# Gated linear attention with a SiLU MLP on one core: attention output with tokens on partitions and turned by transposes, results stored from ScalarE's queue

## The chip, the core and the metric

One NeuronCore of a Trainium2 chip runs the whole program. Its engines work side by side, each with its own instruction stream: TensorE (PE; its weight loads are listed apart as PEld), VectorE (DVE), ScalarE (ACT), GpSimd (POOL) and SyncE (SP), which here only issues transfers. Sixteen DMA engines move data between HBM and the on-chip memory SBUF; matmuls write to PSUM. The metric is the device time of one execution in microseconds (us), as a median over runs; lower is better.

## The reference

Inputs are q, k, v and f_logit of shape (4, 8, 768, 48), f32, and two weight matrices. What is computed:

```
f = 1.0 / (1.0 + np.exp(-f_logit))
state = np.zeros((B, H, D, D), dtype=np.float32)
for t in range(S):
    state = f[:, :, t, :, None] * state + np.einsum('bhd,bhe->bhde', k[:, :, t], v[:, :, t])
    y[:, :, t] = np.einsum('bhd,bhde->bhe', q[:, :, t], state)
x = y.transpose(0, 2, 1, 3).reshape(B * S, H * D)      # (3072, 384)
h = x @ w_in                                           # (3072, 2048)
g = h * (1.0 / (1.0 + np.exp(-h)))
out = g @ w_out                                        # (3072, 384)
```

## The kernel before

The 768 tokens are cut into six chunks of 128. Chunk g holds four units, one per batch entry b, and a unit is all eight heads of that entry. Heads are paired (four pairs) in most matmuls. For a chunk the work is:

- **prep(g)**: `logs` takes exp and log of the gate logits on ACT; `decay` sums the logs over the tokens by a matmul with a triangle of ones (tile `cs`, one PSUM buffer), takes two exponentials of the sum on ACT (`ia`, then `a`), and multiplies k by `ia` on POOL (`ki`) and q by `a` on DVE (`qg`). `values` converts v to bf16, and `lasts` gives the decay of the whole chunk (`al`).
- **attend(g)**, unit by unit and staggered: `transposes` (T) turns qg and ki by eight PE transposes and copies them out on DVE (`qk`); `scores` (A) makes the score tiles, which DVE masks into `atm`; `outputs` (Y) makes the attention output; `state` (D) updates the running state `st`.
- **mlp_in(g)** multiplies by w_in, 48 matmuls in 16 groups of three, each group followed by one SiLU on ACT (`hT`). **mlp_out(g)** multiplies by w_out, four tiles of 16 matmuls, recorded in groups of four; each finished tile is copied to `o_sb` (three buffers) and stored.

In `outputs` before, the result has features on partitions: `y_ps` is [128 features, 3, 128 tokens]. For each of the three feature blocks the kernel multiplies the heads that overlap the block; v sits zero-padded in `vp` (each head in a window of D + 128 columns) so that heads which straddle a block edge add only their own features, and `st` is kept at the full width of 384 columns with zeros off its diagonal blocks. A unit needs 10 matmuls against v and, from chunk 1 on, 6 against the state, all with 128 columns. One DVE copy makes `xT`, the operand of mlp_in.

The order of the work is written by hand: `run` interleaves generators, always taking the next step of the stream that has used the smallest share of its declared cost (`T_COST`, `A_COST`, `Y_COST`, `D_COST`, 650 for a group of the MLP, 200 for a unit of prep). Each engine then executes its own list strictly in that order. Chunk 1 is special: its first two units (FIRST) and its last two (SECOND) are handled apart, since their data still arrives while the MLP of chunk 0 runs. Names such as `logs(1, *SECOND)` say chunk and half.

All loads are issued from SP. In the kernel before, the stores of the results (L280) are issued from SP too, in program order among the loads; the weights come through POOL's queue (`load_w_in`, `load_w_out`). An engine's DMA instruction stands in its list like any other: what follows it waits until it has been issued.

PSUM tiles that matter: `cs`/`al_ps` share one buffer, `a_ps` and `t_ps` have one each, `y_ps` and `d_ps` share two ("yd"), `h_ps` and `o_ps` share two.

Of the kernel before, what the change touches and what calls it, by code (L numbers as in the profile page):

```python
# [41 lines left out]
def kernel(  # L42
# [20 lines left out]
    VW = D + 128  # L63
# [34 lines left out]
    vp = [singles.tile([C, B, 128 + H * VW], BF16, name=f"vp{i}") for i in range(2)]  # L98
    st = [singles.tile([C, NP, HD], BF16, name=f"st{i}") for i in range(B)]
# [93 lines left out]
    def outputs(g, b):  # L193
        i = g % 2
        y_ps = yps.tile([128, KT, C], F32, name="y_ps", tag="yd")
        for t in range(KT):
            terms = []
            if g > 0:
                for p in range(NP):
                    if 2 * D * p < 128 * (t + 1) and 2 * D * (p + 1) > 128 * t:  # L200
                        terms.append((st[b][:, p, 128 * t:128 * (t + 1)], qkT[b][:, 0, p, :]))
            for h in range(H):
                if D * h < 128 * (t + 1) and D * (h + 1) > 128 * t:
                    terms.append((v_window(i, b, h, t), atm[b][:, h % 2, h // 2, :]))
            for n, (l, r) in enumerate(terms):
                nc.tensor.matmul(y_ps[:, t, :], l, r, start=(n == 0), stop=(n == len(terms) - 1))  # L206
# [4 lines left out]
    def state(g, b):
        i = g % 2
        flat = st[b].rearrange("p n w -> p (n w)")
        blocks = bass.AP(flat.tensor, flat.offset, [list(flat.ap[0]), [HD + 2 * D, NP], [1, 2 * D]])
        d_ps = yps.tile([128, NP, 2 * D], F32, name="d_ps", tag="yd")
        if g > 0:
            nc.tensor.matmul(d_ps, ident, blocks, start=True, stop=False, skip_group_check=True)  # L217
        vv = v_data(i, b)
        for p in range(NP):
            nc.tensor.matmul(d_ps[:, p, :], ki[i][:, b, 2 * p:2 * p + 2, :], vv[:, 2 * p:2 * p + 2],  # L220
# [218 lines left out]
```

## Time and profile before

| what | us |
|---|---|
| median of 3 runs (lowest, highest) | 245.88 (244.97, 246.54) |
| the profiled execution's own time | 248.17 |
| its span, first to last instruction | 246.4 |
| PE / ACT / DVE / POOL busy in the span | 201.1 / 114.3 / 111.0 / 53.3 |
| mean granted TensorE clock | 0.924 of full speed |

The span is what the trace shows; 1.77 us of the execution lie around it. Times in the trace count from the span's start. A granted clock of 1.00 is 2.4 GHz, and 0.5 is 1.2 GHz. A busy PE is a union of overlapping matmuls, so what a matmul costs in a stream is read from the distance between starts, not from its own duration (a lone matmul's duration contains its way through the array).

### The profile page before, as it was taken

The page shows a single profiled execution, that of the slowest core. Times are in us where ns is not written, and L with a number is a line of the kernel's source. Part 1 is how long each engine was busy: PE and PEld are TensorE (multiplying, and loading weights), DVE is VectorE, ACT ScalarE, POOL GpSimd, SP SyncE. Part 2 cuts the span into 40 slices and gives each one's busy share as a digit, 9 for nine tenths or more (in the row PEclk, how much of TensorE's full clock was granted, in tenths as well). Part 3 has the DMA queues.
Part 4 walks back from the last instruction along what each step waited for, and adds up shares of the span by engine and source line. Part 5 has one row for each costly group of instructions (what it writes and reads, how often), then busy time and mean ns, then how long its engine had stood idle before and what let it go on. Part 6 is the DMA issues. An engine that isn't in the chain of part 4 may idle for free.

```text
span 246.4 us, 4049 instructions
## 1 busy us (share of the span) xinstructions
PE 201.1 (82%) x1680; PEld 123.4 (50%) x1680; DVE 111.0 (45%) x193; ACT 114.3 (46%) x181; POOL 53.3 (22%) x65
## 2 busy tenths in 40 slices
PE   0346689968604896899779999999999999999994
PEld 0125534536304672687535565655666555663462
DVE  7727722246204544467655345763557453520011
ACT  4351237850410386348265683556735654008600
POOL 8629100050300006300190000900009100000000
PEclk9999769999965798589958999999999999999999
DMA  8999999999992000699409991179601100100011
GB/s 138 187 186 194 191 185 190 197 180 185 189 192 95 0 3 32 131 188 176 85 28 195 187 137 49 49 141 188 90 35 64 36 0 0 63 37 32 3 64 64
DMA packets 105971, 27.00 MB, mean 110 GB/s; under 512 B 99296, under 2 KB 105952, under 8 KB 105952
## 3 DMA queue, kind: packets, MB, share of 16 engines
q1 hardware_dynamic: 102272, 23.60, 60.3%
q0 software_dynamic: 3680, 3.15, 7.9%
q8 instruction: 13, 0.21, 0.4%
q14 instruction: 6, 0.05, 0.1%
HBM read 25.17 MB, written 4.72 MB: 121 GB/s over the span
## 4 chain that ended last, share of the span: by engine, by line
PE 77%; DMA 6%; DVE 5%; ACT 4%; SPq 4%; issue 2%; ACTq 0%; DVEq 0%
PE h_ps L263 29%; PE o_ps L273 25%; PE y_ps L206 9%; PE t_ps L176 5%; SPq L85 4%; PE a_ps L186 3%; DMA out_dram<-o_sb 3%; DMA q_ld<-in_q_dram 3%; DVE atm L190 2%; ACT ia L144 2%; PE cs L142 2%; ACT a L147 2%; PE d_ps L220 2%; DVE qk L178 1%; PE d_ps L217 1%
## 5 line engine op out<-in xcount | busy, mean ns | idle before, releaser
L266 ACT ACTIVATE hT<-h_ps 128x512 bf16<-128x512 f32 x96 | 57.3, 597 | 64.0 <-PE h_ps L263 62.0
L263 PE MATMUL h_ps<-xT,w_in_sb 128*128 128x512 bf16 (+1 forms) x336 | 79.6, 373 | 0.9 <-DVE xT L209 0.7
L273 PE MATMUL o_ps<-w_out_sb,hT 128*128 128x384 bf16 x384 | 72.0, 330 | 0.0
L273 PEld LDWEIGHTS <-hT 128*128 128x128 bf16 x384 | 35.9, 99 | 27.7 <-issue 7.2
L263 PEld LDWEIGHTS <-w_in_sb 128*128 128x128 bf16 x336 | 32.6, 104 | 29.5 <-issue 9.0
L145 POOL TENSOR_TENSOR ki<-k_ld,ia 128x384 bf16<-128x384 f32 x24 | 26.3, 1094 | 67.5 <-ACT ia L144 26.8
L190 DVE TENSOR_TENSOR atm<-a_ps,triu 128x512 bf16<-128x512 f32 x48 | 30.9, 685 | 17.6 <-PE a_ps L186 17.4
L278 DVE COPY o_sb<-o_ps 128x384 f32<-128x384 f32 x24 | 13.4, 556 | 44.9 <-PE o_ps L273 32.5
L155 POOL CAST vp<-v_ld 128x384 bf16<-128x384 f32 x22 | 15.1, 691 | 70.3 <-DMA v_ld<-in_v_dram 70.3
L144 ACT ACTIVATE ia<-cs 128x384 f32<-128x384 f32 x24 | 11.8, 490 | 33.2 <-PE cs L142 33.2
L148 DVE TENSOR_TENSOR qg<-q_ld,a 128x384 bf16<-128x384 f32 x24 | 17.9, 754 | 16.9 <-ACT a L147 12.0
L178 DVE COPY qk<-t_ps 128x1024 bf16<-128x1024 bf16 x24 | 16.6, 690 | 18.0 <-PE t_ps L176 18.0
L142 PE MATMUL cs<-lf,triu 128*128 128x384 bf16 x24 | 8.9, 369 | 18.5 <-ACT a L147 10.2
L206 PE MATMUL y_ps<-atm,vp 128*128 128x128 bf16 x240 | 23.7, 234 | 0.1
L224 DVE TENSOR_TENSOR st<-d_ps,al 48x192 bf16<-48x192 f32 x40 | 14.2, 354 | 21.0 <-PE d_ps L220 17.0
L176 PE MATMUL t_ps<-ident,qg 128*128 128x128 bf16 x96 | 11.3, 252 | 15.0 <-DVE qg L148 11.7
L176 PEld LDWEIGHTS <-qg 128*128 128x128 bf16 x96 | 8.8, 115 | 21.6 <-DVE qg L148 13.8
L209 DVE CAST xT<-y_ps 128x384 bf16<-128x384 f32 x24 | 13.3, 555 | 12.3 <-PE y_ps L206 12.3
L206 PEld LDWEIGHTS <-vp 128*128 128x128 bf16 x240 | 17.8, 106 | 0.5 <-issue 0.5
L206 PE MATMUL y_ps<-qk,st 128*128 128x128 bf16 x120 | 16.5, 219 | 0.0
L186 PE MATMUL a_ps<-qk 48*128 48x128 bf16 x192 | 10.2, 230 | 6.0 <-DVE atm L190 6.0
L186 PEld LDWEIGHTS <-qk 48*128 48x128 bf16 x192 | 5.8, 99 | 15.5 <-issue 7.7
(37 smaller groups left out, 126.6 us busy)
## 6 DMA issues: line engine op xcount, KB each, us to landing
out_dram<-o_sb SPq DMA_DIRECT2D x24, 192.0 KB, 1.9
f_ld<-in_f_logit_dram SPq DMA_DIRECT2D x4, 768.0 KB, 11.0
k_ld<-in_k_dram SPq DMA_DIRECT2D x4, 768.0 KB, 6.4
q_ld<-in_q_dram SPq DMA_DIRECT2D x4, 768.0 KB, 10.1
v_ld<-in_v_dram SPq DMA_DIRECT2D x4, 768.0 KB, 11.1
f_ld<-in_f_logit_dram SPq DMA_DIRECT2D x4, 384.0 KB, 6.7
k_ld<-in_k_dram SPq DMA_DIRECT2D x4, 384.0 KB, 6.7
q_ld<-in_q_dram SPq DMA_DIRECT2D x4, 384.0 KB, 6.8
```

What stands on the lines that cost most here:

```text
L144: nc.scalar.activation(ia, cs, AF.Exp, scale=1.0)
L145: nc.gpsimd.tensor_mul(ki[i][:, b, :, 0:D], loaded[g, "k"][:, b], ia)
L148: nc.vector.tensor_mul(qg[i][:, b, :, 0:D], loaded[g, "q"][:, b], a)
L155: nc.gpsimd.tensor_copy(dst, src)
L176: nc.tensor.transpose(t_ps[:, j, p, :], src[i][:, b, 2 * p:2 * p + 2, :], ident)
L178: nc.vector.tensor_copy(sb, t_ps)
L186: nc.tensor.matmul(a_ps[:, r, p, :], qkT[b][lo:lo + D, 1, p, :], qkT[b][lo:lo + D, 0, p, :], start=True, stop=True)
L190: nc.vector.tensor_mul(sb[:, r], a_ps[:, r], triu[:, None, :].to_broadcast([C, NP, C]))
L206: nc.tensor.matmul(y_ps[:, t, :], l, r, start=(n == 0), stop=(n == len(terms) - 1))
L263: nc.tensor.matmul(h_ps[:, j], w_in_sb[:, kk, (n + j) * 128:(n + j + 1) * 128], xT[g][:, kk, lo:hi].rearrange("p b c -> p (b c)"), start=( ...
L266: nc.scalar.activation(hT[g][:, n:n + per, lo * C:hi * C], h_ps, AF.Silu)
L273: nc.tensor.matmul(o_ps, hT[g][:, n, b * C:(b + 1) * C], w_out_sb[:, n, :], start=(n == 0), stop=(n == NT - 1))
```

## The change

`outputs` now makes the attention output with tokens on partitions: `y_ps` is [128 tokens, 8 heads, 48]. Per pair there is one matmul against the state (moving operand `st`, 96 columns, from chunk 1 on) and two against v (moving operand `vb`, 48 columns). The result is copied to SBUF as bf16 (`y`), and a new step `turn` (X) makes three PE transposes of it into `x_ps` and copies these to `xT`. In `attend`, X of a unit stands one round after its Y. `vp` becomes the plain `vb`, `st` shrinks to 96 columns per pair, and their zero fills go or move to POOL.

The copy of each result tile and its store move to ACT (`nc.scalar.copy`, `nc.scalar.dma_start`), so that SP issues loads alone. In the opening, the first half runs through its scores before the second half's decays, the copies of chunk 0's outputs are ACT's, and both weights are requested in one place. The declared costs of prep rise from 320 to about 1000 per unit, and some leads are set anew.

```diff
-    vp = [singles.tile([C, B, 128 + H * VW], BF16, name=f"vp{i}") for i in range(2)]
-    st = [singles.tile([C, NP, HD], BF16, name=f"st{i}") for i in range(B)]
+    vb = [singles.tile([C, B, H, D], BF16, name=f"vb{i}") for i in range(2)]
+    st = [singles.tile([C, NP, 2 * D], BF16, name=f"st{i}") for i in range(B)]
...
+    def outputs(g, b, engine=None):
         i = g % 2
-        y_ps = yps.tile([128, KT, C], F32, name="y_ps", tag="yd")
+        y_ps = yps.tile([C, H, D], F32, name="y_ps", tag="yd")
+        opened = False
+        for p in range(NP):
+            if g > 0:
+                nc.tensor.matmul(y_ps[:, 2 * p:2 * p + 2, :], qkT[b][:, 0, p, :], st[b][:, p, :],
+                                 start=not opened, stop=False, skip_group_check=True)
+                opened = True
+            for r in range(2):
+                nc.tensor.matmul(y_ps[:, 2 * p + r, :], atm[b][:, r, p, :], vb[i][:, b, 2 * p + r, :],
+                                 start=not opened, stop=True, skip_group_check=True)
+                opened = True
+        sb = wk.tile([C, HD], BF16, name="y")
+        evac(engine, sb, y_ps.rearrange("p h d -> p (h d)"))
+        ysb[b] = sb
+
+    def turn(g, b, engine=None):
+
+        x_ps = yps.tile([128, KT, C], BF16, name="x_ps", tag="yd")
         for t in range(KT):
...
+            nc.tensor.transpose(x_ps[:, t, :], ysb[b][:, 128 * t:128 * (t + 1)], ident)
...
+        evac(engine, xT[g][:, :, b, :], x_ps)
...
-            nc.vector.tensor_copy(o_sb, o_ps)
+            nc.scalar.copy(o_sb, o_ps)
             r0 = b * S + g * C
-            nc.sync.dma_start(out=out[r0:r0 + C, :], in_=o_sb)
+            nc.scalar.dma_start(out=out[r0:r0 + C, :], in_=o_sb)
...
-            yield 200.0
+            yield 1000.0
...
+        for b in range(*FIRST):
+            transposes(0, b)
         logs(0, *SECOND)
         for b in range(*FIRST):
+            scores(0, b)
+        for b in range(*SECOND):
+            decay(0, b)
+        load_w_in()
+        load_w_out()
+        for b in range(*FIRST):
+            outputs(0, b, nc.scalar)
+        for b in range(*SECOND):
             transposes(0, b)
...
-        load(2, "f")
-
-
-        run((mlp_in(0, *ALL), mlp_cost(*ALL)), (states(0, *ALL), B * D_COST))
-        for name in "kqv":
+        for name in "fkqv":
             load(2, name)
         load(3, "f")
+
+
+        run((mlp_in(0, *ALL), mlp_cost(*ALL)), (states(0, *ALL), B * D_COST))
...
-        run((part(out0, 3900.0), 3900.0))
+        run((part(out0, 5850.0), 5850.0))
         run((part(out0, 1950.0), 1950.0), (prep(1, *FIRST), prep_cost(*FIRST)))
-        run((out0, mlp_cost(*ALL) - 5850.0), (attend(1, *FIRST), attend_cost(1, *FIRST)))
+        run((out0, mlp_cost(*ALL) - 7800.0), (attend(1, *FIRST), attend_cost(1, *FIRST)))
...
-            (chain(wait(3000.0), prep(2, *ALL)), 3000.0 + prep_cost(*ALL)))
+            (chain(wait(1000.0), prep(2, *ALL)), 1000.0 + prep_cost(*ALL)))
...
-                lead = half if g == 1 else 1300.0
+                lead = half if g == 1 else 2000.0
```

SP's list from the loads of chunk 2 on, before:

```order
L85 DMA f_ld<-in_f_logit_dram 128x32x48
L85 DMA k_ld<-in_k_dram 128x32x48
L85 DMA q_ld<-in_q_dram 128x32x48
L85 DMA v_ld<-in_v_dram 128x32x48
L85 DMA f_ld<-in_f_logit_dram 128x32x48
L280 DMA out_dram<-o_sb 128x384 x6
L85 DMA k_ld<-in_k_dram 128x32x48
```

and the same place in the change (the last two rows are loads of chunk 3):

```order
L84 DMA f_ld<-in_f_logit_dram 128x32x48
L84 DMA k_ld<-in_k_dram 128x32x48
L84 DMA q_ld<-in_q_dram 128x32x48
L84 DMA v_ld<-in_v_dram 128x32x48
L84 DMA f_ld<-in_f_logit_dram 128x32x48
L84 DMA k_ld<-in_k_dram 128x32x48
L84 DMA q_ld<-in_q_dram 128x32x48
```

Before, the first six stores stand behind the gate logits of chunk 3 and ahead of k of chunk 3; in the change no store stands in this list.

ACT's list from the prep of chunk 1's first half to that of its second half (`logs` is the pair e, lf), before:

```order
L124 ACT_TABLE_LOAD
L135 ACTIVATE e<-f_ld 128x768
L136 ACTIVATE lf_101<-e 128x16x48
L144 ACTIVATE ia<-cs 128x384
L147 ACTIVATE a<-cs 128x384
L144 ACTIVATE ia<-cs 128x384
L147 ACTIVATE a<-cs 128x384
L165 ACTIVATE al<-al_ps 128x8
L135 ACTIVATE e<-f_ld 128x768
L136 ACTIVATE lf_101<-e 128x16x48
L144 ACTIVATE ia<-cs 128x384
```

and in the change, from the second stored tile of chunk 0 on:

```order
L288 COPY o_sb<-o_ps 128x384
L290 DMA out_dram<-o_sb 128x384
L137 ACTIVATE ia<-cs 128x384
L140 ACTIVATE a<-cs 128x384
L137 ACTIVATE ia<-cs 128x384
L140 ACTIVATE a<-cs 128x384
L288 COPY o_sb<-o_ps 128x384
L290 DMA out_dram<-o_sb 128x384
L158 ACTIVATE al<-al_ps 128x8
L288 COPY o_sb<-o_ps 128x384
L290 DMA out_dram<-o_sb 128x384
L128 ACTIVATE e<-f_ld 128x768
```

The logs of the second half (e, lf) stood right behind al; they now stand behind the copies and stores of the third and the fourth result tile of chunk 0, and a copy waits until PE has finished its tile.

DVE's list in the opening, before:

```order
L148 TENSOR_TENSOR qg_103<-q_ld,a 128x8x48 x2
L178 COPY qk<-t_ps 128x1024 x2
L148 TENSOR_TENSOR qg_103<-q_ld,a 128x8x48 x2
L190 TENSOR_TENSOR atm<-a_ps,triu 128x512 x4
L209 CAST xT<-y_ps 128x3x128 x2
L178 COPY qk<-t_ps 128x1024 x2
L190 TENSOR_TENSOR atm<-a_ps,triu 128x512 x4
L209 CAST xT<-y_ps 128x3x128 x2
```

and in the change:

```order
L141 TENSOR_TENSOR qg_103<-q_ld,a 128x8x48 x2
L171 COPY qk<-t_ps 128x1024 x2
L183 TENSOR_TENSOR atm<-a_ps,triu 128x512 x4
L141 TENSOR_TENSOR qg_103<-q_ld,a 128x8x48 x2
L171 COPY qk<-t_ps 128x1024 x2
L183 TENSOR_TENSOR atm<-a_ps,triu 128x512 x4
```

The first half's four masks (atm) now stand ahead of the second half's two qg, and the four copies to xT are no longer in DVE's list.

## Rows read from the trace of the kernel before

**Rows 1.** The page: clock and DMA share in 40 slices of 6.16 us.

```profile
PEclk9999769999965798589958999999999999999999
DMA  8999999999992000699409991179601100100011
```

**Rows 2.** Timeline, opening, DVE and PE: start us, us, instruction, [idle before, releaser].

```profile
17.54 1.82 DVE L148 TENSOR_TENSOR qg<-q_ld,a 128x384 bf16<-128x384 f32 x2 [3.41 <-DMA q_ld<-in_q_dram]
19.28 1.27 DVE L190 TENSOR_TENSOR atm<-a_ps,triu 128x512 bf16<-128x512 f32 x2
...
31.66 1.44 PE L263 MATMUL h_ps<-xT,w_in_sb 128*128 128x512 bf16 x3 [0.65 <-DVE xT L209]
```

**Rows 3.** Line L114, the two loads of w_out: issue durations, starts, time to landing.

```profile
L114 POOL DMA_DIRECT2D w_out_sb<-in_moe_w_out_dram x2: 881/897/913, 22.1 to 23.0; - x2
DMA to landing us min/median/max: 16.3/18.6/20.8
```

**Rows 4.** Timeline, 45 to 80 us: SP's issues, and what waits for them.

```profile
45.27 4.71 PE L273 MATMUL o_ps<-w_out_sb,hT 128*128 128x384 bf16 x28
...
63.74 4.22 SPq L85 DMA_DIRECT2D f_ld<-in_f_logit_dram  x1
...
75.15 0.56 DVE L278 COPY o_sb<-o_ps 128x384 f32<-128x384 f32 x1 [11.92 <-DMA out_dram<-o_sb]
...
77.11 0.61 PE L176 MATMUL t_ps<-ident,qg 128*128 128x128 bf16 x4 [9.64 <-DVE qg L148]
```

**Rows 5.** Chain that ended last: start us, us, what (starts within it give spacings).

```profile
59.77 1.30 PE o_ps L273 x8
...
61.40 0.89 PE y_ps L206 x16
...
99.06 0.41 PE al_ps L161 x16
...
134.13 0.45 PE t_ps L176 x8
```

**Rows 6.** Timeline of PE: the state's matmuls and the next start.

```profile
63.59 0.33 PE L220 MATMUL d_ps<-vp,ki 128*128 128x96 bf16 x4
63.77 0.33 PE L142 MATMUL cs<-lf,triu 128*128 128x384 bf16 x1
...
65.11 0.32 PE L142 MATMUL cs<-lf,triu 128*128 128x384 bf16 x1 [1.02 <-ACT a L147]
```

**Rows 7.** Lines: busy us, mean ns of one | idle before, releaser.

```profile
L144 ACT ACTIVATE ia<-cs 128x384 f32<-128x384 f32 x24 | 11.8, 490 | 33.2 <-PE cs L142 33.2
L278 DVE COPY o_sb<-o_ps 128x384 f32<-128x384 f32 x24 | 13.4, 556 | 44.9 <-PE o_ps L273 32.5 <-DMA out_dram<-o_sb 11.9
```

**Rows 8.** Timeline of ACT: the SiLUs' end and the logs of chunk 2.

```profile
88.01 0.60 ACT L266 ACTIVATE hT<-h_ps 128x512 bf16<-128x512 f32 x1 [0.95 <-PE h_ps L263]
88.62 1.28 ACT L124 ACT_TABLE_LOAD   x1
...
91.43 1.48 ACT L136 ACTIVATE lf<-e 128x1536 bf16<-128x1536 f32 x1
```

**Rows 9.** Stretches: length, busy us (count) of PE, PEld, DVE, ACT, POOL, clock, DMA share, GB/s.

```profile
99.40:112.90 13.50, 12.72 (x129) 9.93 (x127) 7.35 (x13) 5.90 (x10) 1.49 (x2) 0.72 1.18 174
112.90:128.20 15.30, 12.24 (x126) 8.14 (x125) 9.47 (x17) 8.66 (x14) 6.49 (x8) 0.86 0.49 81
...
175.90:192.20 16.30, 15.89 (x157) 10.67 (x155) 9.74 (x19) 9.80 (x14) 7.13 (x8) 1.00 0.10 38
```

**Rows 10.** Timeline of PE: first group of mlp_in of chunks 2 and 3.

```profile
128.03 1.48 PE L263 MATMUL h_ps<-xT,w_in_sb 128*128 128x512 bf16 x3
...
160.57 0.81 PE L263 MATMUL h_ps<-xT,w_in_sb 128*128 128x512 bf16 x3
```

**Rows 11.** Line L280, the stores: issue ns (min/median/max), time to landing.

```profile
L280 SPq DMA_DIRECT2D out_dram<-o_sb x24: 332/333/4727, 68.0 to 243.6; - x24
DMA to landing us min/median/max: 1.8/1.9/7.0
```

More of the change, by code (lines that the diff above doesn't have):

```diff
@@ L62 @@
     MT = B * C
-    VW = D + 128
     singles = ctx.enter_context(tc.tile_pool(name="singles", bufs=1))
@@ L191, in scores @@
         atm[b] = sb
-    def outputs(g, b):
-        i = g % 2
-        y_ps = yps.tile([128, KT, C], F32, name="y_ps", tag="yd")
-        for t in range(KT):
[L197 to L206, printed above, removed]
+    ysb = {}
@@ new lines, in evac @@
+    def evac(engine, dst, src):
+        if engine is nc.scalar:
+            nc.scalar.copy(dst, src)
+        else:
+            nc.vector.tensor_copy(dst, src)
+    def outputs(g, b, engine=None):
+        i = g % 2
+        y_ps = yps.tile([C, H, D], F32, name="y_ps", tag="yd")
[12 more added lines that the diff above has]
+        ysb[b] = sb
@@ L214, in state @@
-        blocks = bass.AP(flat.tensor, flat.offset, [list(flat.ap[0]), [HD + 2 * D, NP], [1, 2 * D]])
         d_ps = yps.tile([128, NP, 2 * D], F32, name="d_ps", tag="yd")
         if g > 0:
-            nc.tensor.matmul(d_ps, ident, blocks, start=True, stop=False, skip_group_check=True)
-        vv = v_data(i, b)
+            nc.tensor.matmul(d_ps, ident, st[b], start=True, stop=False, skip_group_check=True)
         for p in range(NP):
-            nc.tensor.matmul(d_ps[:, p, :], ki[i][:, b, 2 * p:2 * p + 2, :], vv[:, 2 * p:2 * p + 2],
+            nc.tensor.matmul(d_ps[:, p, :], ki[i][:, b, 2 * p:2 * p + 2, :], vb[i][:, b, 2 * p:2 * p + 2],
@@ L223, in state @@
             lo = 64 * r
-            nc.vector.tensor_mul(blocks[lo:lo + D, :, r * D:(r + 1) * D],
+            nc.vector.tensor_mul(st[b][lo:lo + D, :, r * D:(r + 1) * D],
                                  d_ps[lo:lo + D, :, r * D:(r + 1) * D],
                                  alast[g][lo:lo + D, b, :, None].to_broadcast([D, NP, D]))
-    T_COST, A_COST, Y_COST, D_COST = 450.0, 350.0, 900.0, 330.0
+    T_COST, A_COST, Y_COST, D_COST, X_COST = 450.0, 350.0, 400.0, 330.0, 170.0
     def attend(g, lo, hi):
         units = range(lo, hi)
-        for s in range(len(units) + 2):
+        for s in range(len(units) + 3):
             if s < len(units):
@@ L239, in attend @@
                 yield A_COST
-            if s >= 2:
+            if 2 <= s <= len(units) + 1:
                 outputs(g, units[s - 2])
@@ L245, in attend @@
                     yield D_COST
+            if s >= 3:
+                turn(g, units[s - 3])
+                yield X_COST
     def attend_cost(g, lo, hi):
-        return (hi - lo) * (T_COST + A_COST + Y_COST + (D_COST if g < NCH - 1 else 0.0))
+        return (hi - lo) * (T_COST + A_COST + Y_COST + X_COST + (D_COST if g < NCH - 1 else 0.0))
     hT = {}
@@ L290, in prep @@
             decay(g, b)
-            yield 200.0
+            yield 1000.0
         lasts(g, lo, hi)
-        yield 120.0 * (hi - lo)
+        yield 100.0
     def prep_cost(lo, hi):
-        return (hi - lo) * 320.0
+        return (hi - lo) * 1000.0 + 100.0
     def wait(cost):
@@ L337 @@
             values(0, b)
+        for b in range(*FIRST):
+            transposes(0, b)
         logs(0, *SECOND)
         for b in range(*FIRST):
-            transposes(0, b)
+            scores(0, b)
         for b in range(*SECOND):
             decay(0, b)
+        load_w_in()
+        load_w_out()
         for b in range(*FIRST):
-            scores(0, b)
-        load_w_in()
-        for b in range(*FIRST):
-            outputs(0, b)
+            outputs(0, b, nc.scalar)
         for b in range(*SECOND):
             transposes(0, b)
+        for b in range(*FIRST):
+            turn(0, b, nc.scalar)
         for b in range(*SECOND):
             values(0, b, nc.scalar)
-        load_w_out()
         for span in (FIRST, SECOND):
@@ L359 @@
         for b in range(*SECOND):
-            outputs(0, b)
+            outputs(0, b, nc.scalar)
+        for b in range(*SECOND):
+            turn(0, b, nc.scalar)
         for t in (lf[1], qg[1], ki[1], lf[2]):
             nc.gpsimd.memset(t[:, :, :, D:64], 0.0)
-        load(2, "f")
-        run((mlp_in(0, *ALL), mlp_cost(*ALL)), (states(0, *ALL), B * D_COST))
-        for name in "kqv":
+        for name in "fkqv":
             load(2, name)
         load(3, "f")
+        run((mlp_in(0, *ALL), mlp_cost(*ALL)), (states(0, *ALL), B * D_COST))
         exp_ln_tables()
```

13 lines of the change are left out of this document (2 added, 11 removed).

## The prediction

> **What bounds the kernel now.** I read the clock by slices first, then the stretches between stages, then the chain of waits, and last the timelines around the longest pauses. The clock row shows a program that runs at full clock only from about 135 us on: around 70, 100 and 125 us whole slices stand at 5 to 8 tenths [rows 1]. Where the clock is full, PE is the bound: from 175.90 to 192.20 it is busy 15.89 of 16.30 us [rows 9]. From 99.40 to 128.20 it is busy 24.96 (12.72 + 12.24) of 28.80 us at a granted clock of 0.72 and 0.86. So there are two sums to make: matmul work that is removed, which counts everywhere, and pauses before 130 us, which cost their own length and then a stretch at 1.2 GHz.
>
> The longest pause ends at 77.11: PE waited 9.64 us for qg of chunk 1's second half. DVE had that work, but stood 11.92 us in the copy of the fourth result tile, which needed its buffer back from a store, and the store stood in SP's list behind a load that was issued from 63.74 to 67.96 [rows 4]. In the opening, 31.66 us pass before the first matmul of the MLP; DVE stands 3.41 us for the second half's q, does the two qg and then still has the first half's masks and copies [rows 2].
>
> **The matmuls.** Starts give the price in a stream: 16 of 128 columns take 0.89 us (56 ns each), eight transposes 0.45 us (56 ns), sixteen of one column 0.41 us (26 ns, each with its own weight load) [rows 5], four of 96 columns 0.18 us (45 ns) [rows 6]. A unit's Y is 16 x 56 ns = 0.89 us now. In the change it is four of 96 columns (0.18) and eight of 48. No row has 48 columns; between one column (26 ns) and 96 (45 ns) I take 28, since half of 128's 56 is 28 too: 0.22. With X, three transposes (0.17), a unit is 0.57, a gain of 0.32 (bounds 0.34 and 0.19). Twenty units have the state: 6.4 us, spread below by stage.
>
> **Copies.** DVE gives up 24 copies of 556 ns and gets 24 of the same size for `y` [rows 7]: nothing, since it is busy 9.74 of 16.30 us where the clock is full [rows 9]. ACT gets 24 copies, priced by its own 128x384 exponential from PSUM, 490 ns [rows 7], and 24 issues of 332 ns [rows 11]. That is 0.82 us a tile, and four tiles on top of 9.80 us in a stretch of 16.30 leave ACT below the bound [rows 9]. But ACT works in order, so I follow what stands behind these steps. The POOL fills that go lie beside loads under way: nothing.
>
> **Stage by stage, against the span of 246.40.**
> - Opening to the first h_ps (31.66). The first half's masks, 2 x 1.27 us, move into DVE's 3.41 us pause, and two copies (2 x 0.56) leave DVE: -3.6 [rows 2, 7]. At the end stand y's copy, X and a second copy on ACT instead of one copy on DVE: +0.6. Sum -3.0 (bounds -1.0 and -4.0: DVE's chain gone only in part, or the turn hidden).
> - mlp_in(0) keeps its 13.6 us (31.66 to 45.27), so mlp_out(0) starts at about 42.3 and needs the second half of w_out 1.3 us later, at 43.6 (eight of its matmuls take 1.30 us [rows 5]). That load is issued at 23.0 and lands by 43.8 [rows 3], in the change 0.8 later, since the second half's cs stands behind both scores. +1.0 (bounds 0 and +1.3).
> - 45.27 to 77.11 (31.8 us). The wait for qg goes, -9.6 [rows 4]; Y of two units, -0.7. New: the second half's logs stand on ACT behind the copy and store of the fourth tile, so they start about 1.2 us after PE has finished that tile (0.49 + 0.33 and two handovers). They are two passes over half of the columns that take 1.48 us each for a whole chunk [rows 8], so at least 1.5 us. Of these 2.7 us PE covers 0.7 with the last D (0.34) and two X (0.34), and then cs must wait: +2.0. Only three groups of mlp_out are left between attend's steps, where there were seven: +0.4. Sum -7.9.
> - 77.11 to 99.40. Y of two units -0.7. At 1.2 GHz the first 6 us lost half of it before; a shorter pause ahead leaves 2 us of loss where there were 4: -2.0. New: the logs of chunk 2 end 4.3 us after the last SiLU (88.62 to 92.91) [rows 8], and with a lead of 1000 in place of 3000 only 2.4 us of PE's work stand ahead of the first cs: +1.7. Sum -1.0.
> - 99.40 to 128.03. By the clock of 0.72 and 0.86 up to 5.9 us are lost to 1.2 GHz ((1 - 0.72) x 13.5 + (1 - 0.86) x 15.3) [rows 9]. With prep spread (1000 a unit), PE no longer waits 1.02 us at each of four cs in a row [rows 6], so it stays busier: I take back 4.5, and 1.6 of the 3.1 us of idle in 112.90 to 128.20. Y of four units -1.3. New: al, a table load (1.28) and the first SiLU (0.60) [rows 8] now stand behind a copy and a store, and al comes right before mlp_in, so the third group of mlp_in waits about 1.0. Sum -6.4.
> - Chunks 2 to 4: Y -3.8; the first group of chunk 2 took 1.48 us, that of chunk 3 0.81 [rows 10], and some 1.3 us there go; smaller prep waits -0.6. Against it the wait at mlp_in's start three times, +3.0, and 0.2 each for the last xT behind the last qg on DVE. Sum -2.1.
> - Chunk 5's MLP and the last store: a 0.49 us copy for one of 0.56. 0.
>
> Total -3.0 + 1.0 - 7.9 - 1.0 - 6.4 - 2.1 = -19.4: a span of 227.0, an execution of 228.8 with the 1.77 us around it. The median of the runs shown lies 2.29 below the profiled execution, so I forecast **226.5 us**.
>
> **Rivals.**
> - *The stores wait for SP's loads on ACT.* An issue of a store took 332 ns at the median, but up to 4.73 us [rows 11], and the loads ahead of it 4.22 us each [rows 4]. Of the 16 loads of a whole chunk's tile, five were issued by 67.96; eleven more of 4.2 us would keep SP issuing until about 114 in the change, where nothing else is in its list (an estimate), and the eight stores of chunks 0 and 1 fall into that time. If a store's issue on ACT stands until SP's is done, that is 2.1 us on average, half of it on PE's path: 8 x 1.05 = +8, **234.5**. For it: these rows. Against it: the long store issues may be SP's own queue being full. Chance 0.22. The Trainium skill (Perfetto Trace Analysis, on HWDGE DMA instructions) says that the descriptor generator is shared by the issuing sequencers and locked for exclusive use until all descriptors of an instruction have been generated; by that page this rival would hold, and no row here can show it, since only SP issues.
> - *The new waits don't bind.* If the logs, the SiLUs and w_out are never late and the clock stays at 1.00 from the first MLP on, 1.0 + 2.4 + 1.7 + 1.0 + 3.6 and 2 us of leftover 1.2 GHz go, 11.7 in all: **215**. For it: chunk 3 ran so. Chance 0.20.
> - *The change doesn't free the buffer.* The store has its own queue, yet the transfers meet on the same DMA engines, busy at 9 tenths until about 74 us [rows 1]; a store landed in up to 7.0 us instead of 1.9 [rows 11]. With three buffers the fourth copy, some 12 us after the first, would be late only if landing took over 10. Then the 7.9 of the third stage go: **234.5**. Chance 0.05. The Trainium skill (DMA: Bandwidth & Descriptors, on issuing engines) says that issuing from several engines saves only the time of issuing; by that page alone 5 x 0.33 = 1.7 us would be saved there. The trace shows more, an order in one list that held a store until 68.
> - *Slower.* ACT's list is PE's feed. If each of the eight stores holds ACT for a whole load of 4.2 us and PE with it, 8 x 4.2 = 33.6 outweighs 19.4: **260**. It decides at 2.4 us a store. Against it: mlp_out's matmuls need nothing from ACT for 2.6 us at a time. Chance 0.03.
> - Two of these together, with the clock low up to 130 us: no change, 0.03.
>
> **The numbers.** The forecast holds 0.47. Its own range is 220 to 231; reaching down over the second rival and up over the first and third it is **213 to 237**, which leaves out the two last cases and what lies beyond the sized terms, some 0.15. One per cent, 2.5 us, is about what runs of this kernel tell apart. Faster by over 1%: 0.47 + 0.22 + 0.20 + 0.05 = 0.94; within 1% 0.03; slower 0.03.
>
> **What would show it.** Right: 0.57 us for Y and X of a unit where PE runs at full clock, no wait of o_sb for a store, PE's pause near 70 us under 3 us, a first h_ps near 28.7, cs waiting for lf at about 60 us, and a clock row at 9 from slice 16 on. Wrong: store issues on ACT of over 1 us (first rival), h_ps waiting on w_in or w_out for more than 1.5 us, or a clock still at 5 to 7 after 100 us.

## The result and the profile after

The changed kernel takes **225.64 us** (median of 4 runs, 225.35 to 228.28) against 245.81 for the kernel before on the same chip: a ratio of **0.9205** (95% interval 0.913 to 0.928). The forecast was 226.5 in a range of 213 to 237. The profiled execution took 225.62 us with a span of 223.8, and its granted clock was 0.991 where the kernel before had 0.924. Over all measurements here the kernel before took 241.8 to 248.2 us at granted clocks from 0.971 down to 0.924; its profiled execution is the slowest of them, ratios are taken from the faster runs and medians from all, and differences against its profile are too large by 2.3 us (against the median above) to about 5.

The page of the kernel after, busy times and then clock and DMA share in 40 slices of 5.6 us, against [rows 1]:

```profile
PE 186.7 (83%) x1664; PEld 111.7 (50%) x1664; DVE 101.2 (45%) x180; ACT 128.1 (57%) x213; POOL 49.8 (22%) x68
...
PEclk9999999999997999999999999999999999999999
DMA  8999999999999999999899011000011000110011
```

One slice is left below 9, at 67 to 73 us, where [rows 1] has four dips: the three that the prediction names, and one at 25 to 37 us. PE is busy 186.7 us where it was 201.1: of the 14.4 us some 6.8 are the cheaper Y (20 units of 0.34), most of the rest is the same work at 2.4 instead of 1.2 GHz. ACT carries 13.8 us more, DVE 9.8 less.

Timelines of the kernel after (start us, us, instruction, [idle before, releaser]), the opening and the turn from chunk 0 to chunk 1, against [rows 2, 4, 6]:

```profile
17.36 1.83 DVE L141 TENSOR_TENSOR qg<-q_ld,a 128x384 bf16<-128x384 f32 x2 [0.99 <-DMA q_ld<-in_q_dram]
...
27.58 1.44 PE L273 MATMUL h_ps<-xT,w_in_sb 128*128 128x512 bf16 x3 [0.57 <-ACT xT L190]
...
43.83 5.36 PE L283 MATMUL o_ps<-w_out_sb,hT 128*128 128x384 bf16 x32 [0.83 <-DMA w_out_sb<-in_moe_w_out_dram]
...
59.69 4.10 SPq L84 DMA_DIRECT2D v_ld<-in_v_dram  x1
...
60.40 0.48 ACT L288 COPY o_sb<-o_ps 128x384 f32<-128x384 f32 x1 [7.77 <-PE o_ps L283]
60.91 0.34 ACTq L290 DMA_DIRECT2D out_dram<-o_sb  x1
61.29 0.84 ACT L128 ACTIVATE e<-f_ld 128x768 f32<-128x768 f32 x1 [0.42 <-ACT o_sb L288]
62.16 0.84 ACT L129 ACTIVATE lf<-e 128x768 bf16<-128x768 f32 x1
63.06 0.32 PE L135 MATMUL cs<-lf,triu 128*128 128x384 bf16 x1 [1.19 <-ACT lf L129]
...
67.08 0.63 PE L169 MATMUL t_ps<-ident,qg 128*128 128x128 bf16 x4
```

DVE's wait for the second half's q shrank from 3.41 to 0.99 us, since the first half's masks stand in it, and the first h_ps comes 4.1 us earlier. The transpose that ended a 9.64 us pause at 77.11 now starts at 67.08 with no wait. In its place stands the wait that the prediction named: cs waits 1.19 us for the logs, which stand on ACT behind the fourth tile's copy and store. The store at 60.91 was issued in 0.34 us in the middle of a load's issue on SP (59.69 to 63.79).

Lines after (the stores' issue ns; the copies' busy us, mean ns | idle before, releaser) and timelines, against [rows 11, 7, 5, 8, 10]:

```profile
L290 ACTq DMA_DIRECT2D out_dram<-o_sb x24: 338/339/374, 45.8 to 221.0; - x24
```

```profile
L288 ACT COPY o_sb<-o_ps 128x384 f32<-128x384 f32 x24 | 11.5, 478 | 32.7 <-PE o_ps L283 32.7
L192 DVE CAST y<-y_ps 128x384 bf16<-128x384 f32 x20 | 11.0, 551 | 2.8 <-PE y_ps L205 2.8
L192 DVE COPY xT<-x_ps 128x384 bf16<-128x384 bf16 x20 | 6.9, 356 | 5.7 <-PE x_ps L216 5.3
```

```profile
80.45 0.32 PE L135 MATMUL cs<-lf,triu 128*128 128x384 bf16 x1 [2.62 <-ACT lf L129]
...
119.54 0.21 PE L201 MATMUL y_ps<-st,qk 128*128 128x96 bf16 x1
...
119.92 1.46 PE L273 MATMUL h_ps<-xT,w_in_sb 128*128 128x512 bf16 x6
...
128.32 0.33 PE L216 MATMUL x_ps<-ident,y 128*128 128x128 bf16 x3
128.49 0.81 PE L283 MATMUL o_ps<-w_out_sb,hT 128*128 128x384 bf16 x4
...
140.58 1.28 ACT L276 ACT_TABLE_LOAD   x1
...
140.60 0.81 PE L273 MATMUL h_ps<-xT,w_in_sb 128*128 128x512 bf16 x3 [0.78 <-DVE xT L192]
...
141.69 1.64 PE L273 MATMUL h_ps<-xT,w_in_sb 128*128 128x512 bf16 x6
```

No copy of a result waits for a store any more (24 of 478 ns on ACT, all idle time before them from o_ps), and no store's issue took over 0.374 us, where SP's reached 4.73 [rows 11]. Starts give a unit's Y as 0.38 us (119.54 to 119.92) and its X as 0.17 (128.32 to 128.49): 0.55 against 0.89 before. The largest wait left is 2.62 us, cs for the logs of chunk 2. At the start of chunk 3's MLP h_ps waits 0.78 us for xT, and the six matmuls behind it take 1.64 us instead of 1.46, so the late SiLU costs 0.18.

Stretches after (length, busy us and count of PE, PEld, DVE, ACT, POOL, clock, DMA share, GB/s), the stage in which [rows 9] had 0.72 and 0.86:

```profile
88.31:99.50 11.19, 11.06 (x152) 8.89 (x150) 8.76 (x16) 7.60 (x12) 0.75 (x2) 1.00 1.29 206
99.50:110.66 11.16, 8.45 (x100) 5.28 (x99) 8.92 (x18) 7.59 (x14) 6.94 (x8) 1.00 1.08 181
```

### The profile page after: what moved, and what is told of

It reads as the page before. It is cut to its first block, busy times and chain, and to the rows that moved or that the text cites. A ratio compares the mean times of both kernels' runs of the same rounds, so it can differ in the third digit from the quotient of the medians.

```text
span 223.8 us, 4048 instructions
## 1 busy us (share of the span) xinstructions
PE 186.7 (83%) x1664; PEld 111.7 (50%) x1664; DVE 101.2 (45%) x180; ACT 128.1 (57%) x213; POOL 49.8 (22%) x68
## 4 chain that ended last, share of the span: by engine, by line
PE 62%; DMA 12%; ACT 11%; DVE 8%; issue 2%; POOL 2%; SPq 1%; ACTq 1%; DVEq 0%
PE h_ps L273 24%; PE o_ps L283 22%; DMA w_out_sb<-in_moe_w_out_dram 9%; PE t_ps L169 5%; DVE qg L141 4%; PE a_ps L179 3%; DMA q_ld<-in_q_dram 3%; ACT ia L137 2%; ACT a L140 2%; PE cs L135 2%; ACT e L128 2%; ACT lf L129 2%; PE y_ps L201 2%; POOL w_in_sb L109 1%; PE y_ps L205 1%
## 5 line engine op out<-in xcount | busy, mean ns | idle before, releaser
L273 PE MATMUL h_ps<-xT,w_in_sb 128*128 128x512 bf16 (+1 forms) x336 | 75.7, 360 | 3.4 <-DVE xT L192 2.2
L273 PEld LDWEIGHTS <-w_in_sb 128*128 128x128 bf16 x336 | 31.5, 101 | 31.1 <-issue 10.8
L138 POOL TENSOR_TENSOR ki<-k_ld,ia 128x384 bf16<-128x384 f32 x24 | 25.2, 1049 | 94.1 <-ACT ia L137 93.1
L141 DVE TENSOR_TENSOR qg<-q_ld,a 128x384 bf16<-128x384 f32 x24 | 23.3, 974 | 31.5 <-ACT a L140 23.1
L288 ACT COPY o_sb<-o_ps 128x384 f32<-128x384 f32 x24 | 11.5, 478 | 32.7 <-PE o_ps L283 32.7
L171 DVE COPY qk<-t_ps 128x1024 bf16<-128x1024 bf16 x24 | 16.5, 689 | 21.1 <-PE t_ps L169 21.1
L148 POOL CAST vb<-v_ld 128x384 bf16<-128x384 f32 x22 | 16.3, 744 | 25.0 <-DMA v_ld<-in_v_dram 25.0
L128 ACT ACTIVATE e<-f_ld 128x768 f32<-128x768 f32 (+1 forms) x8 | 9.3, 1163 | 6.9 <-DMA f_ld<-in_f_logit_dram 6.5
L192 DVE CAST y<-y_ps 128x384 bf16<-128x384 f32 x20 | 11.0, 551 | 2.8 <-PE y_ps L205 2.8
L205 PE MATMUL y_ps<-vb,atm 128*128 128x48 bf16 x192 | 11.7, 189 | 0.4 <-DVE atm L183 0.4
L205 PEld LDWEIGHTS <-atm 128*128 128x128 bf16 x192 | 10.0, 100 | 3.7 <-issue 2.1
```

The costliest lines, as they stand in the source:

```text
L138: nc.gpsimd.tensor_mul(ki[i][:, b, :, 0:D], loaded[g, "k"][:, b], ia)
L141: nc.vector.tensor_mul(qg[i][:, b, :, 0:D], loaded[g, "q"][:, b], a)
L171: nc.vector.tensor_copy(sb, t_ps)
L205: nc.tensor.matmul(y_ps[:, 2 * p + r, :], atm[b][:, r, p, :], vb[i][:, b, 2 * p + r, :], start=not opened, stop=True, skip_group_check=True)
L273: nc.tensor.matmul(h_ps[:, j], w_in_sb[:, kk, (n + j) * 128:(n + j + 1) * 128], xT[g][:, kk, lo:hi].rearrange("p b c -> p (b c)"), start=( ...
```

## The experiments

All differences below are read from one measure, the stages between first starts of matmuls on PE in the profiled executions: the first o_ps of chunk 0, the first h_ps of chunk 1's second half, the first h_ps of chunk 2, the end. What was said above of the profile of the kernel before holds for its row here.

```
                       to o_ps(0)  to h_ps(1,SECOND)  to h_ps(2)  to the end   span   clock
before                   45.27         54.06            28.70       118.37     246.4  0.924
after                    41.54         46.77            22.35       113.14     223.8  0.991
after, once more         41.75         47.95            22.35       113.15     225.2  0.985
before, ACT stores       45.94         45.86            25.48       119.72     237.0  0.978
before, new Y            46.09         51.11            23.58       114.92     235.7  0.957
before, both             46.16         44.79            23.64       115.61     230.2  0.978
after, old stores        41.70         59.63            23.21       115.36     239.9  0.949
after, DVE copies        41.95         49.33            24.48       117.44     233.2  0.978
after, SP list reordered 41.60         47.05            21.58       114.27     224.5  0.977
after, logs early        42.05         47.56            22.35       113.24     225.2  0.985
after, old prep costs    41.46         47.32            23.64       117.28     229.7  0.968
merged prep              41.63         42.79            22.36       115.12     221.9  0.985
 + w_out, last xT        41.95         41.43            21.90       113.42     218.7  1.000
 + logs of chunk 2       41.89         40.69            21.97       113.35     217.9  1.000
```

**The parts alone, on the kernel before.** First the copy and store:

```diff
-            nc.vector.tensor_copy(o_sb, o_ps)
+            nc.scalar.copy(o_sb, o_ps)
-            nc.sync.dma_start(out=out[r0:r0 + C, :], in_=o_sb)
+            nc.scalar.dma_start(out=out[r0:r0 + C, :], in_=o_sb)
```

> The kernel before, with one part of the change alone: result tiles are copied and stored by ACT on its own queue. Theory (the store's place in SP's list made the pause): the 9.64 us pause at 77.11 falls under 3 us, and with it the low clock behind it, so 246 - 9.6 - (2 to 5) = 231 to 234. Rival (the pause only moves to the next late thing, the half chunk's data or qg behind other work on DVE): a pause of 5 us or more stays near 70 to 77 us, and the time is 240 or more.

Measured: 239.93 us, ratio 0.980 (0.970 to 0.991), a drop of 4.9 us where 12 to 15 were expected. The pause is gone, but part of it came back as other waits. In the timeline of PE:

```profile
66.96 0.48 PE L142 MATMUL cs<-lf,triu 128*128 128x384 bf16 x1 [2.37 <-ACT lf L136]
68.76 0.48 PE L142 MATMUL cs<-lf,triu 128*128 128x384 bf16 x1 [1.32 <-ACT a L147]
70.26 0.35 PE L161 MATMUL al_ps<-ones,lf 128*128 128x1 bf16 x8 [1.02 <-ACT a L147]
```

The logs of the second half stand behind the fourth tile's copy on ACT here as well, and the cs rows of 0.48 in place of 0.32 show 1.2 GHz. Of the 4.7 us in these three rows 2.7 are new (2.37, and 0.30 of the 1.32); PE waited 1.02 us at the other two places in the kernel before as well [rows 6]. Neither theory had the size. In the profiles the stage with the pause shrinks by 8.2 us, but with it the clock rises from 0.85 to 0.93, so part of the 8.2 is the low clock of that one profile.

Then Y alone (the new `outputs` and `turn` with copies on DVE, stores on SP):

> The kernel before, with the attention output's new form alone (tokens on partitions, three transposes; copies on DVE), stores still in SP's list. Theory (Y is sized by matmul starts, 6.4 us in all, but what it gains ahead of 77 us vanishes in a pause whose end is set by SP's load): 240 to 241.5, the pause still there and longer than 9 us. Rival (fewer, narrower matmuls, or two more handovers per unit, count for more than their starts say): under 238, or over 244.

Measured: 237.45, ratio 0.976 (0.970 to 0.983). The pause stayed, as the theory had it:

```profile
74.97 0.56 DVE L288 COPY o_sb<-o_ps 128x384 f32<-128x384 f32 x1 [11.08 <-DMA out_dram<-o_sb]
...
76.11 1.44 PE L273 MATMUL h_ps<-xT,w_in_sb 128*128 128x256 bf16 x6 [8.95 <-DVE xT L192]
```

The time fell by 5.8 us (0.024 x 244.0), near the 6.4 that the starts gave for Y and inside the drop that was expected, 4.5 to 6 from 246: the kernel before stood at 244 on this chip, and the rival's "under 238" was met for that reason alone. Only two of the twenty units stand ahead of the pause, so it had little to swallow. The stage behind the pause is 5.1 us shorter in the profiles, of which Y explains 1.3; the rest comes with the clock, 0.94 there against 0.80 in the profile of the kernel before, and is not shown to be Y's.

Both together:

> Both of these parts, in the order of the kernel before (old opening, old costs of prep, old leads). Theory: the two add, since the pause no longer swallows Y's share: 246 - 6.4 - (12 to 14) = 226 to 229, and the new order and opening are worth the rest, 0 to 3 us. Rival (the gain comes from the order: spread prep and the opening half by half): 233 or more.

Measured: 232.68, ratio 0.958 (0.951 to 0.964), 10.3 us where 17 to 20 were expected. The parts multiply (0.980 x 0.976 = 0.957). The opening, the order, prep's costs and leads are therefore worth more than expected: another 5.9 us, down to 226.81 (the second measurement of the change, below, on another chip; from 0.958 to 0.933). So the rival, that the order carries the gain, has a part too: its limit, 233 of 246, is a ratio of 0.947, and 0.958 lies above it.

**The change without its stores.** Only the four lines above, turned back:

> The changed kernel, with copies back on DVE and stores back in SP's list. Theory: SP now lists k, q, v of chunk 2 and the gate logits of chunk 3 ahead of the first store, and issues these until 68.7, so the fourth tile's copy ends near 71 in place of 60.9 and the clock falls behind it: 225.6 + 10 to 14 = 236 to 240. Rival (the order in SP's list costs little once prep is spread): under 230.

Measured: **242.83**, ratio 1.000 (0.995 to 1.005). All the rest of the change together is worth nothing without this part. In the timeline:

```profile
63.47 4.12 SPq L84 DMA_DIRECT2D f_ld<-in_f_logit_dram  x1
67.68 7.80 SPq L290 DMA_DIRECT2D out_dram<-o_sb  x4
74.56 0.56 DVE L288 COPY o_sb<-o_ps 128x384 f32<-128x384 f32 x1 [13.68 <-DMA out_dram<-o_sb]
...
75.93 0.50 PE L216 MATMUL x_ps<-ident,y 128*128 128x128 bf16 x3 [14.55 <-DVE st L231]
```

That is more than the 236 to 240 expected. The first store is issued at 67.7, with the new Y alone at 67.8, before at 68.0 [rows 11], whatever PE does, since SP's loads stand ahead of it; a faster opening only makes PE wait longer, 14.55 us. With the new Y, the store part is worth 4.8 us in the old order (237.45 to 232.68) and 16 in the new (242.83 to 226.81, on two chips; from a ratio of 1.000 to 0.933).

**The place in the list, or the engine that issues?** Copies on ACT, stores on SP, the loads of chunk 2 moved behind chunk 0's stores:

```diff
-            nc.scalar.dma_start(out=out[r0:r0 + C, :], in_=o_sb)
+            nc.sync.dma_start(out=out[r0:r0 + C, :], in_=o_sb)
...
-        for name in "fkqv":
-            load(2, name)
-        load(3, "f")
...
         logs(1, *SECOND)
+        for name in "fkqv":
+            load(2, name)
+        load(3, "f")
```

> The changed kernel, copies on ACT, with the stores back in SP's list, and there the loads of chunk 2 and the gate logits of chunk 3 moved behind the four stores of chunk 0. Theory (it is the place in a list executed in order that made the pause, not which engine issues): no pause over 3 us near 60 to 77 us; the loads of chunk 2 now start about 61 in place of 49 and land by 71 (f) to 84 (q), so q may hold DVE for 1 to 2 us near 82: 226 to 231. Rival (the stores need a queue of their own, since SP issues loads without end): a pause of 8 us or more comes back, 236 or more.

Measured: 226.97, ratio 0.933 (0.925 to 0.940), the same as the change (0.921 and 0.933 in two measurements). SP's own rows:

```profile
48.77 12.46 SPq L290 DMA_DIRECT2D out_dram<-o_sb  x4
61.28 0.43 SPq L84 DMA_DIRECT2D f_ld<-in_f_logit_dram  x1
```

```profile
L290 SPq DMA_DIRECT2D out_dram<-o_sb x24: 332/333/2986, 48.8 to 221.7; - x24
```

So the pause came from the order in one list, not from the engine: SP may issue the stores if they stand ahead of loads that can wait. (The copies are ACT's here and DVE's in the change without its stores; what was waited for there, 13.68 us, was a store.) q was not late near 82; that part of the expectation fell. What ACT's own queue buys is that nobody has to find this order.

**Who copies.** The change beside itself and with the copies back on DVE, stores still on ACT's queue:

> The changed kernel once more, as the measure for the three beside it: 225.6, between 224.5 and 227.

Measured: 226.81 (226.15 to 228.79), ratio 0.933 (0.925 to 0.942).

```diff
-            nc.scalar.copy(o_sb, o_ps)
+            nc.vector.tensor_copy(o_sb, o_ps)
```

> The changed kernel with the copies of the results back on DVE, the stores still on ACT's queue. Theory (what counts is that the stores left SP's list, not who copies): 225 to 228, no pause over 3 us; ACT's store waits for DVE's copy, so what stands behind it starts no earlier. Rival (ACT's 24 copies of 0.48 us are a cost, since ACT feeds PE): under 224. Rival (DVE is full in attend's stages): over 229.

Measured: **235.77**, ratio 0.969 (0.962 to 0.977), 9 us slower than the change. The theory fell. ACT's and PE's timelines:

```profile
62.68 0.84 ACT L128 ACTIVATE e<-f_ld 128x768 f32<-128x768 f32 x1 [9.14 <-DVE o_sb L288]
```

```profile
146.98 0.81 PE L273 MATMUL h_ps<-xT,w_in_sb 128*128 128x512 bf16 x2 [1.10 <-DVE xT L192]
...
149.95 0.81 PE L273 MATMUL h_ps<-xT,w_in_sb 128*128 128x512 bf16 x3 [1.07 <-ACT hT L276]
```

A store on ACT cannot be issued before DVE has copied, and DVE copies only behind what stands ahead in its list (qg, masks, y); what stands behind the store on ACT (logs, al, SiLU) then waits for DVE. Most of the 9.14 us is PE's, though: ACT idled 7.77 us for the same tile in the change. What it costs shows at 149.95, where PE waits 1.07 us for ACT's hT.

The second rival said that DVE is full. Its number came true (over 229), its reason did not. From chunk 3's first h_ps to the end all of these kernels run at a granted clock of 1.00, and there the two places can be told apart:

```
                          copies  stores   chunk 3's first h_ps to the end, us
after, old stores          DVE     SP       82.65
before, new Y              DVE     SP       82.82
after, SP list reordered   ACT     SP       82.67
after                      ACT     ACT      83.20
after, once more           ACT     ACT      83.22
after, DVE copies          DVE     ACT      86.22
```

With the stores on SP it makes no difference here who copies. Copy on DVE and store on ACT costs 3.0 us against the change. The other 5 to 6 us lie in the stages before, where the clocks differ as well (0.90 and 0.93 to chunk 1's second half), and are not parted. DVE was busy 112.9 us, 48% of the span.

**Where ACT's logs stand.**

```diff
         logs(1, *FIRST)
+        logs(1, *SECOND)
...
-        logs(1, *SECOND)
```

> The changed kernel, with the logs of chunk 1's second half recorded right behind those of its first half, ahead of the copies of chunk 0's results. Theory (cs waits 1.19 us at 63.06 only because these logs stand behind the fourth tile's copy and store): that wait goes, and the first matmul of chunk 1's MLP comes 1.2 us earlier, 224 to 224.6. Rival (the logs only move ACT's 1.7 us ahead of the first copy, and PE then waits for o_ps): 225.5 or more, with a wait of o_ps on ACT near 47 us.

Measured: 226.30, ratio 0.929 (0.920 to 0.937), no difference from the change beside it. The 1.19 us wait did go, but in this profile PE waited 1.46 us for w_out where it was 0.59 in the run beside it; over eight profiles of kernels with the same opening this wait lay between 0.59 and 2.02. No wait of o_ps on ACT, as the rival has it, is in the trace. Inconclusive in the time; the row that is gone shows the mechanism.

**The costs that spread prep.**

```diff
-            yield 1000.0
+            yield 200.0
         lasts(g, lo, hi)
-        yield 100.0
+        yield 120.0 * (hi - lo)
...
-            (chain(wait(1000.0), prep(2, *ALL)), 1000.0 + prep_cost(*ALL)))
+            (chain(wait(3000.0), prep(2, *ALL)), 3000.0 + prep_cost(*ALL)))
...
-                lead = half if g == 1 else 2000.0
+                lead = half if g == 1 else 1300.0
```

> The changed kernel with prep's declared cost back at 320 a unit and the leads back at 3000 and 1300. Theory (spreading prep takes away the waits of cs for a, some 1 us at each of several cs in a row): the stretch from chunk 2's MLP to the end grows from 113.1 by about 2.5, the one ahead of it by 1.3, and the 2.62 us wait of cs for the logs of chunk 2 shrinks by about 1: 228 to 229.5. Rival (these costs move waits but take none away): 225 to 226.5.

Measured: 230.73, ratio 0.940 (0.927 to 0.953), an interval that does not part it from the change; the stages do. The stage ahead of chunk 2 is 1.3 us longer, as expected, but not for the reason given: PE's waits there are the same in sum (3.0 and 3.1 us in the run beside it), as the rival said, and the granted clock is 0.93 where the change has 1.00. The three kernels made from the kernel before, which have the old costs too, show 0.93 or 0.94 in this stage. The wait of 2.62 us for the logs is gone, not shorter by 1. From chunk 2 to the end it is 4.1 us longer (2.5 expected): 1.8 in chunk 2, at a clock of 0.95, and 2.3 behind it. Two rows, of ACT and of PE, show a part that was not expected there:

```profile
145.26 1.28 ACT L276 ACT_TABLE_LOAD   x1 [0.40 <-ACT o_sb L288]
...
147.20 0.81 PE L273 MATMUL h_ps<-xT,w_in_sb 128*128 128x512 bf16 x3 [1.12 <-ACT hT L276]
```

This is the wait for the first SiLU that the prediction put into the changed kernel. With the old costs it is there, 1.12 us at two chunks. It hangs on ACT having the copies and stores: from chunk 3's first h_ps to the end the old costs take 85.52 us with these on ACT (here, and in "before, both") and 82.82 without ("before, new Y").

**A version that beats both.** Three steps, each on top of the one before. First the second half's prep beside the first half's attention:

```diff
-        run((part(out0, 5850.0), 5850.0))
+        run((part(out0, 3900.0), 3900.0))
         run((part(out0, 1950.0), 1950.0), (prep(1, *FIRST), prep_cost(*FIRST)))
-        run((out0, mlp_cost(*ALL) - 7800.0), (attend(1, *FIRST), attend_cost(1, *FIRST)))
         logs(1, *SECOND)
-        run((prep(1, *SECOND), prep_cost(*SECOND)))
+        run((out0, mlp_cost(*ALL) - 5850.0), (attend(1, *FIRST), attend_cost(1, *FIRST)),
+            (chain(wait(1000.0), prep(1, *SECOND)), 1000.0 + prep_cost(*SECOND)))
```

> The changed kernel with chunk 1's second half prepared beside the attention of its first half: one group of three fewer tiles' groups of mlp_out(0) ahead of prep (3900 for 5850, so seven groups are left as cover), the logs of the second half right behind the first half's prep, and its prep as a third stream. Theory (the waits of cs at 63 to 66 us, 1.19 + 1.02 + 1.02, and the uncovered waits of attend, 0.78 + 1.39 + 0.39, are what this stage still loses): the stretch from the first o_ps to chunk 1's first h_ps falls from 24.2 to 20 to 22 us, the time from about 226 to 222.5 to 224.5. Rival (DVE is what holds this stage, and two more qg of about 1 us stand in it): no gain, 226 or more.

Measured: **222.20**, ratio 0.915 (0.911 to 0.920). From the first o_ps to chunk 1's first h_ps it takes 21.1 us (41.63 to 62.73) in place of 24.4. The rival's wait shows too, y_ps for DVE's y, 1.46 us, but it is smaller than what went.

Then w_out in four pieces and the last xT on ACT:

```diff
-        for n in range(0, NT, 8):
-            nc.gpsimd.dma_start(out=w_out_sb[:, n:n + 8, :], in_=src[:, n:n + 8, :])
+        for n in range(0, NT, 4):
+            nc.gpsimd.dma_start(out=w_out_sb[:, n:n + 4, :], in_=src[:, n:n + 4, :])
...
-                turn(g, units[s - 3])
+                turn(g, units[s - 3], nc.scalar if s == len(units) + 2 else None)
```

> The same, and two small waits taken away: w_out is loaded in four pieces in place of two (PE waited 0.59 to 0.83 us for its second half), and the last unit's xT is copied by ACT in attend (h_ps waited 0.64 to 0.78 us, three times, for an xT that stood behind qg on DVE). Theory: 2 to 3 us less than the first of these three, 220 to 222. Rival (the pieces land no earlier since the DMA engines are full, and ACT's copy delays al and the SiLU behind it): within 1 us of it.

Measured: **220.82**, ratio 0.912 (0.905 to 0.919). w_out's wait is gone. xT's fell from 0.64 to 0.19 at chunk 2 and only from 0.77 to 0.51 at chunks 3 and 4, where it is now another unit's copy on DVE, and the SiLU behind it costs 0.27 at each. The step is 1.4 us, about half of the theory, and the intervals overlap.

Then the logs of chunk 2 ahead (edit: its `load(2, "f")` between k and q of chunk 1's second half, `logs(2, *ALL)` right behind `logs(1, *SECOND)`):

> The second, and the logs of chunk 2 taken out of the way of its prep: its gate logits are loaded ahead of q and v of chunk 1's second half, and their exp and log are done on ACT behind those of chunk 1's second half, where ACT idled 7.77 us. Theory (cs waited 2.62 us at 80.4 for these logs): that wait goes, another 2 to 3 us, 217 to 220. Rival (q and v of the second half now land later, and T waits for qg): 1 us less or none, with a wait of DVE for q_ld near 60 us.

Measured: **220.42** (219.21 to 223.4), ratio **0.906** (0.901 to 0.912), 0.4 us from the one before. The wait of 2.61 at cs went and that stage shrank by 2.8 us (62.45 to 83.38, now 64.42 to 82.58), but the logs delay ACT's a for chunk 1, DVE's qg then stands ahead of a mask, and PE waits earlier:

```profile
58.46 0.32 PE L135 MATMUL cs<-lf,triu 128*128 128x384 bf16 x1 [1.07 <-ACT a L140]
...
60.80 0.20 PE L201 MATMUL y_ps<-st,qk 128*128 128x96 bf16 x1 [2.03 <-DVE y L192]
```

It is the fastest kernel here; its ratio makes it some 23 us faster than the kernel before. The rival had the size (1 us less or none) but not the cause: near 60 us DVE does not wait for q_ld.

## Why the prediction was right, step by step

```
step                                    predicted   measured (before to after)
opening to first h_ps                     -3.0        -4.1   31.66 to 27.58
first h_ps to 77.11 (now 67.08)           -6.9        -5.95  45.45 to 39.50
  of it the wait for w_out                +1.0        +0.83
to the MLP of chunk 1's second half       -1.0        -1.0   22.22 to 21.23
to chunk 2                                -6.4        -6.35  28.70 to 22.35
chunks 2 to 4                             -2.1        -5.4   92.47 to 87.08
chunk 5 and the end                        0          +0.2
sum of spans                             -19.4       -22.6
```

- **The mechanism was the one named**, the buffer behind a store behind SP's loads. The change without its stores, and the reordered list, show it from both sides: 14.55 us of pause with the stores behind the loads, no wait over 2.7 us with them ahead or on ACT's queue.
- **Opening.** The masks did move into the wait for q (3.41 to 0.99); the gain was 1.1 larger than taken, just past the far bound; what the rest of it is stays open.
- **The third stage** came out 1.0 short, though its waits did as said: the pause is gone, PE waits 1.19 for the logs plus 0.67 for a state update just ahead (2.0 predicted), and all of PE's waits in the stage fell by 6.45 us (14.48 to 8.03) where the sum had 6.2. What is missing lies in busy time: mlp_in(0), which "keeps its 13.6", took 13.96 (27.58 to 41.54), and chunk 1's first h_ps stood at a clock of 0.56.
- **The new wait at chunk 2's logs** was under-sized, 2.62 for 1.7, and the clock there gave back what that cost: 4.2 us were lost to it before (0.81 over 22.22 us) and 1.2 after, 3.0 where 2.0 were taken.
- **To chunk 2**: granted clock 1.00 in both stretches, as the sum had it. PE's busy time fell by 5.35 us, Y's 1.4 and 4.0 of clock (4.5 predicted), and its waits by 1.0. They fell by less than spreading prep was to save, and not all as described: the trace before has three waits of 1.02 at cs there, not four, and after it PE waits 0.78 twice for a state update and 0.64 for xT.
- **Chunks 2 to 4** gained 3.3 us more than predicted, since two terms were wrong, in opposite directions. The wait for the first SiLU at mlp_in's start (+3.0) measured 0.18 each at chunks 3 and 4 and none at chunk 2. Against that, h_ps is held 0.78 and 0.77 by the last xT, where 0.2 each was predicted. While PE does al and waits there, ACT gets through the last copy and store: its table load begins with the first h_ps (140.58 and 140.60). With the old prep costs it begins 1.08 us behind it (145.26 and 144.18), and the 1.12 us wait is there. PE's waits and breaks at cs in chunks 2 and 3 went, about 1.5 us by starts (0.6 predicted), and Y gave 4.1 for 3.8; some 0.7 us stay open.
- **Y and X**: 0.55 a unit for 0.57 predicted; alone it is worth 2.4% (1.7 to 3.0), 5.8 us for 6.4 (clock and pause included). The guess of 28 ns for a matmul of 48 columns was near: with 45 for 96 columns, 0.38 leaves 25.
- **Copies at nothing** held, and only as a balance: DVE gives up 24 o_sb and 24 xT of 0.56 and gets 20 y of 0.55 and 20 xT of 0.36, 9 us less. The result tiles' copies could have stayed on DVE at no cost in chunks 3 to 5, but only with the stores off ACT; with ACT waiting for them, the kernel lost 9 us.
- **The first rival**, stores that wait on ACT for SP's issues, is refuted: 24 issues of 0.338 to 0.374 us, one of them wholly inside a 4.10 us issue of SP. The Trainium skill (Perfetto Trace Analysis, HWDGE DMA instructions) speaks of an exclusive lock; no delay of that size shows in any store here. In SP's own list the store's issue can still be long (2.99 in the reordered list).
- **The second rival** (the new waits don't bind, 215) fell: they bind at cs (1.19 and 2.62) and at w_out (0.83).
- **The third rival** (the buffer isn't freed) fell, since no copy waits for a store. By the Trainium skill (DMA: Bandwidth & Descriptors, issuing engines) a second issuing engine would save only issue time; the runs agree once SP's list is in a good order (226.97 against 226.81), and with the stores behind the loads the second queue was worth 16 us.
- The parts are not independent, which the sum hid: in the old order the stores are worth 4.8, and the order without them nothing. The sum came near because it was followed in time, stage by stage, with each new wait placed behind what it stands behind. That it came within 0.9 us is partly luck. Its span was 3.2 us too long (227.0 against 223.8), and the 2.29 taken off at the end hid most of that. That step took the profile's excess over the median off once more, although the stages (2.0 and 4.5) had already taken back the low clock of that profile, which comes with the excess.

## What to carry to other kernels

Follow one list at a time: a transfer that frees a buffer must not stand behind transfers that can wait, and while it does, every gain ahead of it turns into a longer pause. When work moves to another engine, move the copy and its store together, or the issuing engine inherits the wait. A busy share does not price a moved instruction: with the copies on DVE and the stores on SP the last chunks took 82.7 us, with the same copies and the stores on ACT 86.2. What counts is what stands behind the moved instruction, and for whom.

## What the runs showed of the hardware

The granted clock is not fixed by the program alone. The change's runs took 225.4 to 225.7 us at a clock of 0.99 and 228.3 at 0.977. Two kernels show the same within a stage. "Merged prep" and its successor have PE busy 9.05 of 11.70 and 8.01 of 10.20 us in the stretch ahead of chunk 2's MLP, both at 1.00, and yet the next stretch had a clock of 0.60 (mostly 1.2 GHz) in the one and 1.00 (2.4 GHz) in the other:

```profile
95.00:106.70 11.70, 9.05 (x107) 5.69 (x106) 9.51 (x20) 8.11 (x15) 6.84 (x8) 1.00 1.22 195
106.78:111.00 4.22, 4.22 (x20) 2.22 (x20) 0.69 (x1) 2.07 (x3) 0.04 (x1) 0.60 1.15 202
```

```profile
95.00:105.20 10.20, 8.01 (x96) 4.93 (x94) 8.03 (x16) 7.02 (x14) 6.22 (x7) 1.00 1.27 201
105.28:110.00 4.72, 4.63 (x39) 2.47 (x38) 1.51 (x3) 3.84 (x7) 0.50 (x1) 1.00 1.24 199
```

That is 1.7 us (0.4 x 4.2). Just ahead of it PE waited 0.64 us for xT in the first and 0.19 in the second, but in the change it waited 0.64 there too and the clock stayed at 1.00. So a step of 1 to 2 us, such as the last two here, is read from the stage it is in and not from one total. What decides it in a single run stays open.
